# A Fourier-and-MLP layer on one core: block 8, the first transform and all product units in a new hand-written order

## The chip, the core and the metric

The kernel runs on one NeuronCore of a Trainium2 chip. The core has five engines that run side by side and meet only at semaphores: TensorE (PE in the profile, with its weight loads as PEld), VectorE (DVE), ScalarE (ACT), GpSimd (POOL) and SyncE (SP). Each engine takes its instructions strictly in the order in which they were written for it. DMAs are started by an instruction on SP, ACT or POOL and then run by themselves. The metric is device time in microseconds: 1245.67 us is the median of three runs of the kernel before (1245.28 to 1251.84).

## The reference

```python
def _A_ref(x, dft_seq_re, dft_seq_im, dft_hid_re, dft_hid_im):
    a = jnp.einsum("bsd,ed->bse", x, dft_hid_re)
    b = jnp.einsum("bsd,ed->bse", x, dft_hid_im)
    y = jnp.einsum("ts,bse->bte", dft_seq_re, a) - jnp.einsum("ts,bse->bte", dft_seq_im, b)
    return y

def _B_ref(x, w1, w2):
    h = jnp.einsum("bsd,df->bsf", x, w1)
    zero = jnp.zeros_like(h)
    h = jnp.maximum(h, zero)
    return jnp.einsum("bsf,fd->bsd", h, w2)

x = A_x
xn = _layernorm(x, axis=-1)
return x + _A_ref(xn, A_dft_seq_re, A_dft_seq_im, A_dft_hid_re, A_dft_hid_im) + _B_ref(xn, B_w1, B_w2)
```

x is 2048 x 576 in float32, the hidden size of the MLP is 4608, the Fourier matrices are 2048 x 2048 and 576 x 576 (real and imaginary part of each). A layer norm, a two-dimensional Fourier transform written as matrix products, and an MLP with relu are added to x.

## The kernel before

**Numbers.** Every float32 operand is split in a high and a low float16 part, and a product is three float16 products (high x high, high x low, low x high). Before it is split it is scaled by a power of two that is found from its largest magnitude. The large products use a seven-product scheme (Strassen-Winograd) on 2 x 2 blocks, so there are sums of operand blocks to make before the products and sums of product blocks after them.

**Stages.** (1) The start (BLOCK0): x is loaded tile by tile, normalised, split and transposed, and MLP block 0 is computed. (2) MLP blocks 1 to 8 of 512 hidden columns (BLOCK1, BLOCK, BLOCK8), each in four steps of 512 tokens: step t = 4b+g is block b, token group g, so steps 32 to 35 are block 8. Partial outputs are added to a spill area in device memory by DMAs from POOL. (3) The hidden transform: the normalised x times the 576 x 576 Fourier matrix gives the right-hand operands R (16 row blocks, first 0 to 7, later 8 to 15). (4) Sixteen units multiply blocks of the 2048 x 2048 matrices with R: units 0 to 7 with rows 0 to 7, units 8 to 15 with rows 8 to 15. Between units 7 and 8 stands the second half of the hidden transform (TURN).

**What sets the order.** BLOCK0, BLOCK1, BLOCK, BLOCK8 and TURN are strings of words; run and run_block take them one by one, each calling a function that emits a few instructions, and in a hand-written stretch every engine has its instructions in the order of the words. Units 1 to 6 and 9 to 15 are not in the strings: the function unit emits them in a loop, outside the hand-written stretch, and the framework's planner orders them for each engine. Unit 0 is in BLOCK8; units 7 and 8 are in TURN.

**The words.** In an MLP block: `p:t:i:k` is product k of step t, pair i (7 matmuls, L663); `f` copies a product's bank out (ACT L653 or DVE L655, by the tag :A or :V, L685 to L689 where it adds); `h`, `l`, `r`, `x`, `y`, `H`, `L` make relu, sums and the high and low parts of the hidden values (L672 to L710); `m:t:q` is product q of the second weights (12 matmuls, L760); `e` evicts it (L774 on ACT, L776 on DVE, or L778 where it adds); `a` is the DMA that adds it to the spill area (POOL, L785). `F` loads a block of the large Fourier matrix for its scale (SP, L1164, one buffer for all) and `S` has ACT sum its magnitudes (L1171), so an F waits for the S before it.

For the 576 x 576 matrix: `dl` and `dx` load its four quarters and find their maxima, `dR` and `dp` make the scale, and `dL:z:k` loads part k of its real (z=0) or imaginary (z=1) half again (L1105 to L1123). k is 0 or 1 for the main rows and 2 for the last 64 rows; a last part is eight small DMAs on SP (L336, L337), the others are four (L1121). Parts go to two buffers in turn, except dL:1:2, which goes to free columns of dbuf and accs. `dh` (ACT, L1135) and `dw` (DVE, L1141) make high and low parts, `ds` (DVE, L878 to L881) sums.

In the transform: `q:t:z:n` is product n (7 matmuls, L1321), `c` collects it (L1334, L1336, L1338), `rs` makes the sums (L1300 to L1303), `sh` and `sl` the high and low parts of R (ACT L1290, DVE L1294).

In unit n: `u:n:i:0` and `u:n:i:1` are the halves of product i (12 matmuls each, L1414), `cl:n:q` loads block q of its left operand (SP, L1354), `os` sums blocks (DVE, L1376), `oh:m` and `ol:m` split operand m = 7n+i (ACT L951, DVE L955), `ue` evicts (ACT L1428, DVE L1426 or L1430), `ua` sends a result off: in units 0 to 7 by a POOL DMA that adds to the spill area (L1438), in units 8 to 15 by a store from SP (L1442). `lo` reloads the partial outputs (SP, L1402). The left operand has two sets of buffers, by n odd or even; so have the outputs, by the unit's row p.

**The start.** The first weights' half i=0 is loaded in two halves of three DMAs each, all from SP, between the first and the second tile of x (L973, L974 call load_w1_main and load_w1_rest).

Of the kernel before, what the change touches and what calls it, by code (L numbers as in the profile page):

```python
# [146 lines left out]
f:32:1:5:V h:32:0:12 H:32:0 l:32:0:12 a:31:1 dx:2:0 f:32:1:7 L:32:0 m:31:3 p:33:0:1 p:32:1:3
p:32:1:4 p:33:0:2 e:31:3:A h:32:1:11 h:32:1:22 f:32:1:3 f:33:0:1:V m:31:5 r:32:1 e:31:2:A
h:32:1:12 x:32:1 m:31:4 p:33:0:5 p:33:0:6 e:31:5 dx:2:1 e:31:4 y:32:1 l:32:1:22 S:33:0
f:33:0:5:V m:31:6 f:33:0:6:V l:32:1:12 l:32:1:11 p:33:0:3 p:33:0:7 dl:3 F:33:1 f:33:0:2 e:31:6:A  # L150
f:33:0:7 dx:3:1 f:33:0:3 p:33:1:1 p:33:0:4 p:33:1:2 m:32:0 dx:3:0 h:33:0:11 h:33:0:22 H:32:1
h:33:0:12 dR:0 a:31:4 a:31:5 a:31:6 S:33:1 dL:0:0 f:33:1:1:V e:32:0:A r:33:0 dL:0:1 m:32:1
# [12 lines left out]
p:35:0:6 r:34:1 e:33:4 f:35:0:2 dw:0:2:2 x:34:1 f:35:0:6:A dh:0:2:3 p:35:0:5 f:35:0:5:V S:35:0
m:33:5 m:33:6 p:35:0:7 p:35:1:2 dw:0:2:3 e:33:6:A y:34:1 e:33:5 l:34:1:11 l:34:1:12 dL:1:0
F:35:1 dL:1:1 f:35:0:7 a:33:4 p:35:0:3 p:35:1:1 p:35:0:4 m:34:1 f:35:0:3 f:35:1:1:V p:35:1:6
m:34:0 H:34:1 h:35:0:11 h:35:0:22 r:35:0 p:35:1:5 x:35:0 f:35:1:2 y:35:0 L:34:1 f:35:1:6:V
l:35:0:22 p:35:1:7 H:35:0 h:35:0:12 h:35:1:11 e:34:0:A L:35:0 f:35:1:5:V l:35:0:11 p:35:1:3
f:35:1:7 f:35:1:3 e:34:1 p:35:1:4 m:34:2 a:33:5 a:33:6 m:34:3 r:35:1 dh:1:0:0 dh:1:1:0 e:34:2:A  # L170
l:35:0:12 x:35:1 h:35:1:12 dh:1:0:1 dh:1:1:1 e:34:3:A dh:1:2:1 dh:1:2:0 S:35:1 m:34:4 y:35:1
a:34:1 dw:1:0:0 dw:1:1:0 l:35:1:11 e:34:4 dw:1:2:1 m:34:5 dw:1:0:1 e:34:5 l:35:1:12 m:34:6
dw:1:1:1 m:35:0 ds:1:0 ds:1:1 h:35:1:22 e:34:6:A a:34:4 a:34:5 a:34:6 H:35:1 e:35:0:A dh:1:0:2
dh:1:1:3 m:35:1 L:35:1 q:0:0:1 q:0:0:5 e:35:1 l:35:1:22 m:35:2 m:35:3 dh:1:1:2 pm:0 dw:1:2:0
e:35:2:V e:35:3:A a:35:1 m:35:4 ds:1:2 e:35:4 dw:1:1:2 m:35:5 e:35:5 m:35:6 dh:1:2:2 dh:1:0:3
e:35:6:A dh:1:2:3 fs:0 a:35:5 a:35:6 a:35:4 dw:1:2:2 dw:1:0:3 dw:1:1:3 dw:1:0:2 q:0:0:2 q:0:1:1
q:1:0:1 fm:0 cl:0:0 c:0:1:1:V c:0:0:5:A c:0:0:1:A c:0:0:2 dw:1:2:3 q:0:1:2 q:0:1:6 q:0:0:6 pa:0
pb:0 c:0:1:6:A sh:0:11 sl:0:11 c:0:1:2 q:0:1:5 q:0:1:7 c:0:1:5:A c:0:0:6:V q:0:0:3 pc:0 c:0:1:7
c:0:0:3 pd:0 q:0:1:3 q:0:0:7 q:0:1:4 q:1:1:1 c:0:1:3 sh:0:21 sh:2:11 c:1:0:1:A sl:0:21 c:0:0:7
q:0:0:4 sh:2:22 sh:2:21 c:0:1:4:A sl:2:11 q:1:1:5 sl:2:21 sh:0:22 sl:2:22 q:1:0:2 q:1:0:6  # L180
sl:0:22 q:1:1:2 rs:2 c:1:1:1:A c:0:0:4:A c:1:1:5:A rs:0 q:1:1:3 q:1:1:6 sh:2:0 sh:0:0 c:1:1:6:A
c:1:0:6:A sl:2:0 q:1:0:5 q:1:1:7 c:1:0:5:A c:1:1:2 sl:0:0 c:1:1:7 q:1:0:3 q:1:0:7 sh:3:22
# [1381 lines left out]
```

## Time and profile before

| | us |
|---|---|
| median of three runs (lowest, highest) | 1245.67 (1245.28, 1251.84) |
| the profiled execution | 1249.48 |
| its span, first to last instruction | 1247.6 |
| PE busy | 1215.2 |
| DVE busy | 1050.8 |
| ACT busy | 726.4 |
| POOL busy | 214.7 |

The profile is of one execution; its times are microseconds from the first instruction. Block 8 runs from about 700 to 810 us, the first transform to about 866, units 0 to 7 to about 1022, the second transform to about 1074, and the last units to the end. "idle before, releaser" names what ended an engine's wait. The granted clock is the share of TensorE's full clock that the chip allowed; below 1.00 a matmul takes longer, and PE counts as busy all the same.

### The profile page before, as it was taken

The numbers are of one execution on the slowest core, as the hardware profiler recorded it, in microseconds if no ns is written. First come the engines' busy times: TensorE is split into PE (matmuls) and PEld (weight loads), VectorE is DVE, ScalarE is ACT, GpSimd is POOL, SyncE is SP. The second block draws the span as 40 slices with busy tenths as digits, with TensorE's granted clock in tenths as the row PEclk, the third lists the DMA queues.
The fourth block names the chain that finished last, engine by engine and source line by source line (L and its number), as shares of the span: only waits on it lengthen the run. The fifth ranks groups of instructions, "written<-read, shape, count | busy, mean of one in ns | idle before, by whom it ended". The sixth has DMA issues, their size and how long they took to land.

```text
span 1247.6 us, 26034 instructions
## 1 busy us (share of the span) xinstructions
PE 1215.2 (97%) x10394; PEld 995.8 (80%) x10394; DVE 1050.8 (84%) x2029; ACT 726.4 (58%) x1273; POOL 214.7 (17%) x279
## 2 busy tenths in 40 slices
PE   6999999999999999999999998999999999999998
PEld 6856778888888888888888886876777777777777
DVE  7977999988898889888998787989787669887775
ACT  6765776766756667657666565655444445534332
POOL 2651112222122122212111111200111110000000
PEclk9999999999999999999999998999999999999999
DMA  7997568688878777777676776642555631345431
GB/s 224 202 184 169 166 137 162 158 152 158 164 143 166 152 144 163 137 142 162 135 128 136 168 171 137 107 97 72 160 130 132 137 80 42 118 136 180 137 120 34
DMA packets 127051, 175.96 MB, mean 141 GB/s; under 512 B 48337, under 2 KB 88785, under 8 KB 126929
## 3 DMA queue, kind: packets, MB, share of 16 engines
q1 hardware_dynamic: 98256, 122.38, 34.1%
q0 software_dynamic: 28672, 51.92, 28.9%
q8 instruction: 81, 1.33, 0.4%
q14 instruction: 42, 0.34, 0.1%
HBM read 112.53 MB, written 56.62 MB: 136 GB/s over the span
## 4 chain that ended last, share of the span: by engine, by line
PE 75%; DVE 9%; DMA 7%; issue 4%; ACT 2%; POOL 1%; SPq 1%; ACTq 0%; DVEq 0%; POOLq 0%
PE bank L663 25%; PE p L760 24%; PE p L1414 18%; PE pd L1321 7%; DMA out_dram<-accs 2%; DVE cs L955 2%; DMA accs<-in_x_dram 1%; DMA tb<-in_cim_dram 1%; PE p L539 1%; PE p L800 1%; DVE R L1294 1%; DVE accs L1426 1%; DMA f<-in_cim_dram 1%; DMA x<-in_x_dram 0%; DMA f<-in_cre_dram 0%
## 5 line engine op out<-in xcount | busy, mean ns | idle before, releaser
L760 PE MATMUL p<-w2s,h 128*128 128x288 f16 x2688 | 358.2, 286 | 0.8 <-ACT dbuf L774 0.6
L1414 PE MATMUL p<-R,cs 128*128 128x288 f16 x2688 | 332.9, 287 | 7.1 <-DVE accs L1426 3.9
L1414 PEld LDWEIGHTS <-cs 128*128 128x128 f16 x2688 | 263.7, 98 | 75.6 <-issue 8.5
L760 PEld LDWEIGHTS <-h 128*128 128x128 f16 x2688 | 263.3, 98 | 63.6 <-issue 1.1
L663 PEld LDWEIGHTS <-wbuf 128*128 128x128 f16 x1568 | 154.4, 98 | 25.6 <-issue 4.5
L663 PEld LDWEIGHTS <-dbuf 128*128 128x128 f16 x1568 | 153.2, 98 | 24.8 <-issue 4.7
L663 PE MATMUL bank<-xT,wbuf 128*128 128x256 f16 x896 | 112.1, 276 | 4.3 <-ACT s L653 4.3
L951 ACT ACTIVATE cs<-tb,sc_c 128x1024 f16<-128x1024 f32 x56 | 63.4, 1146 | 89.9 <-PE p L1414 57.0
L663 PE MATMUL bank<-xT,dbuf 128*128 128x256 f16 x896 | 109.9, 273 | 1.2 <-ACT accs L653 1.0
L785 POOL DMA_DIRECT2D spill<-dbuf x70 | 61.5, 928 | 165.6 <-DVE dbuf L778 123.2
L663 PE MATMUL bank<-accs,dbuf 128*128 128x256 f16 x672 | 85.9, 273 | 2.4 <-DVE accs L687 1.7
L955 DVE SCALAR_TENSOR_TENSOR cs<-tb,sc_c,cs 128x1024 f16<-128x1024 f32 x56 | 71.1, 1280 | 20.1 <-ACT cs L951 19.7
L663 PE MATMUL bank<-accs,wbuf 128*128 128x256 f16 x672 | 85.8, 273 | 0.0
L710 DVE TENSOR_TENSOR h<-s,h 128x1024 f16<-128x1024 f32 x64 | 77.3, 1216 | 1.8 <-ACT h L704 1.8
L951 ACT ACTIVATE cs<-accs,sc_c 128x1024 f16<-128x1024 f32 x40 | 45.1, 1144 | 54.3 <-PE p L1414 28.7
L704 ACT ACTIVATE h<-s 128x1024 f16<-128x1024 f32 x64 | 66.5, 1049 | 11.3 <-DVE s L701 11.3
L1171 ACT ACTIVATE f<-f 128x1024 f32<-128x1024 f32 x64 | 67.2, 1049 | 4.1 <-DMA f<-in_cre_dram 3.5
L774 ACT ACTIVATE dbuf<-p,c_ub 128x576 f32<-128x576 f32 x63 | 46.4, 737 | 35.1 <-PE p L760 35.1
L672 ACT ACTIVATE h<-accs 128x256 f16<-128x256 f32 x128 | 51.0, 409 | 25.2 <-DVE accs L687 22.8
L785 POOL DMA_DIRECT2D spill<-wbuf x42 | 39.8, 947 | 147.1 <-DVE wbuf L778 119.0
L653 ACT ACTIVATE accs<-bank 128x256 f32<-128x256 f32 x101 | 38.3, 379 | 46.0 <-PE bank L663 19.6
L955 DVE SCALAR_TENSOR_TENSOR cs<-accs,sc_c,cs 128x1024 f16<-128x1024 f32 x40 | 51.0, 1280 | 12.1 <-ACT cs L951 11.8
(224 smaller groups left out, 1886.8 us busy)
## 6 DMA issues: line engine op xcount, KB each, us to landing
spill<-dbuf POOLq DMA_DIRECT2D x80, 288.0 KB, 4.6
f<-in_cre_dram SPq DMA_DIRECT2D x32, 512.0 KB, 4.5
f<-in_cim_dram SPq DMA_DIRECT2D x32, 512.0 KB, 5.2
spill<-wbuf POOLq DMA_DIRECT2D x48, 288.0 KB, 5.5
raw_w<-in_w_dram SPq DMA_DIRECT2D x18, 576.0 KB, 4.7
raw_w<-in_w_dram SPq DMA_DIRECT2D x17, 512.0 KB, 4.6
accs<-in_cim_dram SPq DMA_DIRECT2D x16, 512.0 KB, 5.1
tb<-in_cre_dram SPq DMA_DIRECT2D x16, 512.0 KB, 4.6
```

Of the source, the lines that this page charges most:

```text
L663: nc.tensor.matmul(ps, l, r, start=first and m == 0, stop=m == len(todo) - 1, skip_group_check=not first,)
L672: nc.scalar.activation(next(high_low(q)), SOURCE[q], AF.Relu)
L704: order["s"] = nc.scalar.activation(next(high_low(SUMS)), stage_of(slice(1, 5)), AF.Copy).ins
L710: order["lo"] = nc.vector.tensor_tensor(lo, stage_of(slice(1, 5)), hi, ALU.subtract).ins
L760: nc.tensor.matmul(ps[:, c], h[:, x, qa, c * P : (c + 1) * P], w[:, y, qb], start=first and i == 0 and j == 0, stop=i == NQ - 1 and j == 2 ...
L774: freed(nc.scalar.activation(o, ps, AF.Copy, scale=us[b]))
L785: nc.gpsimd.dma_start(spill[g, row, col], sums[g, row, col], accum_op=ALU.add)
L951: nc.scalar.activation(hi, src, AF.Copy, scale=s)
L955: nc.vector.scalar_tensor_tensor(lo, src, s, hi, ALU.mult, ALU.subtract)
L1171: nc.scalar.activation(f, f, AF.Abs, scale=2.0**-10, accum_out=sums_c[:, n, q : q + 1])
L1321: nc.tensor.matmul(ps, x[:, k, c * P : (c + 1) * P], dsp[z][:, a, y], start=first and m == 0, stop=m == len(PASSES) - 1, skip_group_check= ...
L1414: nc.tensor.matmul(ps, w[:, a, RANK[k]], r[:, c, RIGHT[rq]], start=first and k == 0 and j == 0, stop=k == HK - 1 and j == 2, skip_group_ch ...
```

## The change

The words of BLOCK8 and TURN are put in another order. No product, sum, split or DMA of them is added or taken away, but some copies and evictions change engine between ACT and DVE. The words for units 1 to 6 are added to BLOCK8, and those for units 9 to 15 to TURN, in place of the loops over unit, which goes away with the function operand. dL:1:2 stood ahead of F:34:0 and is now behind F:34:1. One half of the first weights is loaded from ACT's queue. Two functions, total_w1 and cast_w1, and three names for words (ms, mc, rm) are added; no word of this kernel uses them, nor the prefix 0 that the second run function now takes.

```diff
-L:32:1 p:33:1:6 dL:1:2 l:33:0:22 l:33:0:12 dp:0 x:33:0 f:33:1:2 F:34:0 e:32:1 p:33:1:5
...
-h:34:0:11 ds:0:1 h:34:0:22 e:33:0:A l:34:0:22 l:34:0:11 e:32:6:A r:34:0 h:34:0:12 x:34:0 F:34:1
-dL:0:2 p:34:1:5 p:34:1:6 dh:0:2:1 dh:0:2:0 f:34:1:6:A f:34:1:5:A dh:0:1:3 a:32:5 a:32:6 m:33:1
...
-c:5:0:7 rs:4 q:5:0:3 sh:6:0 c:5:1:7 c:5:0:2 sh:5:21 c:5:1:3 q:5:0:4 q:5:1:4 sh:7:22 sh:4:0
-sh:7:21 fx:1 c:5:0:3 c:5:1:4:A sh:5:11 c:5:0:4:A sl:6:0 sl:4:0 sl:5:11 sl:7:22 sh:7:11 sh:5:22
-sl:5:22 sl:5:21 sl:7:21 sl:7:11 rs:5 oh:2 sh:5:0 oh:3 u:0:0:0 u:0:0:1 u:0:1:0 rs:7 ol:2 sl:5:0
-u:0:1:1 sh:7:0 ue:0:0:A sl:7:0 ol:3 os:0:3 u:0:2:0 u:0:2:1 ue:0:2:A oh:4 u:0:3:0 os:0:2 ol:4
...
+dh:0:0:3 f:34:0:5:V a:32:6 dw:0:0:2 m:33:1 dw:0:0:3 S:34:0 f:34:0:2 dL:0:2 p:34:0:3 f:34:0:6:V
+dw:0:1:0 e:33:0:A p:34:0:7 y:33:1 h:34:0:11 e:33:1 H:33:1 p:34:1:2 f:34:0:7 a:33:1 p:34:1:1
+l:34:0:11 h:34:0:22 L:33:1 p:34:0:4 F:34:1 f:34:1:1:A p:34:1:6 f:34:1:2 h:34:0:12 f:34:0:3
+h:34:1:11 ds:0:1 m:33:2 r:34:0 m:33:3 e:33:2:A f:34:1:6:V dL:1:2 x:34:0 dh:0:1:3 m:33:4 dh:0:2:1
+l:34:0:12 e:33:3:A y:34:0 dw:0:1:3 dh:0:1:2 m:33:5 e:33:4 H:34:0 l:34:0:22 a:33:4 dh:0:2:0
...
+c:5:1:3 rs:6 sh:7:21 u:0:0:0 sh:5:21 q:5:0:5 sl:5:21 sh:6:0 c:5:1:7 sl:4:0 q:5:1:4 sh:7:22
+c:5:0:5:A c:5:1:4:A q:5:0:3 sl:6:0 sh:5:22 c:5:0:7 c:5:0:3 q:5:0:4 sl:5:22 sh:7:11 sl:7:22
+sl:7:11 c:5:0:4:A fx:1 sl:7:21 oh:2 u:0:0:1 rs:5 oh:3 u:0:1:0 ue:0:0:A rs:7 sh:5:0 u:0:1:1 ol:2
+sh:7:0 sl:5:0 u:0:2:0 sl:7:0 ol:3 u:0:2:1 cl:1:3 cl:1:1 cl:1:0 os:0:3 cl:1:2 u:0:3:0 oh:6
...
+u:8:2:1 cl:9:0 cl:9:1 cl:9:3 ol:60 cl:9:2 u:8:3:0 cl:10:2 oh:62 ue:8:1 ue:8:2 u:8:3:1 ol:62
...
+u:9:0:1 ol:66 u:9:1:0 ue:9:0 os:9:3 cl:10:3 u:9:1:1 oh:67 cl:11:0 lo:2 u:9:2:0 ue:9:1 oh:68
+ol:67 u:9:2:1 ol:68 u:9:3:0 ue:9:2 oh:69 os:10:0 ua:9:2 u:9:3:1 ol:69 cl:11:2 u:9:4:0 ue:9:3
+oh:70 ol:70 u:9:4:1 os:10:1 u:9:5:0 oh:71 ue:9:4 cl:11:1 ol:71 ua:9:4 u:9:5:1 os:10:2 u:9:6:0
+oh:72 ue:9:5 ol:72 ua:9:5 u:9:6:1 u:10:0:0 ue:9:6 oh:73 cl:11:3 ua:9:6 ol:73 u:10:0:1 os:10:3
+u:10:1:0 ue:10:0 oh:74 cl:12:0 u:10:1:1 ol:74 u:10:2:0 lo:3 oh:75 os:11:0 u:10:2:1 ol:75 ue:10:1
...
-    def load_w1_rest(b, i, r):
+    def load_w1_rest(b, i, r, eng=nc.sync):
...
-        nc.sync.dma_start(dst[:size], bass.AP(src.tensor, src.offset, both))
-        nc.sync.dma_start(dst[size:], src[: 2 * RH].rearrange("(h p) f -> p h f", h=2))
+        eng.dma_start(dst[:size], bass.AP(src.tensor, src.offset, both))
+        eng.dma_start(dst[size:], src[: 2 * RH].rearrange("(h p) f -> p h f", h=2))
...
     for half in range(2):
-        load_w1_main(0, 0, slice(half, half + 1))
-        load_w1_rest(0, 0, half)
+        eng = (nc.sync, nc.scalar)[half]
+        load_w1_main(0, 0, slice(half, half + 1), eng)
+        load_w1_rest(0, 0, half, eng)
...
-    def unit(n):
-        p, kh = units[n]
-        if kh and p + 1 < NP:
-            load_out(p + 1)
-        for i in range(7):
-            m = n * 7 + i
-            block_product(n, i, slice(0, HK))
-            block_evict(n, i)
-            if i == 0 and n + 1 < nu:
-                for q in (0, 2, 1, 3):
-                    load_c(n + 1, q)
-            if m + AHEAD < 7 * nu:
-                operand(m + AHEAD)
-            block_out(n, i)
...
     run(BLOCK8, turn)
-    end_hand()
-    for n in range(1, HK - 1):
-        unit(n)
-    begin()
     run(TURN, turn)
     end_hand()
-    for n in range(HK + 1, 2 * HK):
-        unit(n)
```

More of the change, by code (lines that the diff above doesn't have):

```diff
@@ L147 @@
[L147 to L152, printed above, removed]
@@ L165 @@
[L165 to L170, printed above, removed]
@@ L171 @@
[L171 to L182, printed above, removed]
@@ new lines @@
+h:35:0:22 f:35:0:3 L:34:1 r:35:0 p:35:0:4 p:35:1:5 e:34:1 h:35:0:12 S:35:1 m:34:2 x:35:0 a:34:1
+y:35:0 dL:1:1 m:34:3 l:35:0:22 e:34:2:A f:35:1:1:V f:35:1:2 H:35:0 l:35:0:12 pm:0 m:34:4
+e:34:3:A L:35:0 h:35:1:11 f:35:1:5:A p:35:1:6 e:34:4 p:35:1:3 l:35:1:11 f:35:1:6:A a:34:4
+p:35:1:7 f:35:1:3 r:35:1 m:34:5 f:35:1:7 x:35:1 h:35:1:22 p:35:1:4 e:34:5 m:34:6 l:35:1:22
+dh:1:2:0 a:34:5 y:35:1 h:35:1:12 dw:1:2:0 dh:1:1:1 m:35:0 dh:1:0:1 e:34:6:V dh:1:1:0 l:35:1:12
+a:34:6 dh:1:0:0 m:35:1 dh:1:2:1 dw:1:1:1 dw:1:1:0 H:35:1 dw:1:2:1 dw:1:0:1 q:0:0:1 e:35:0:A
@@ new lines @@
+oh:11 u:1:1:1 cl:3:0 ol:11 u:1:2:0 oh:12 ue:1:1 ua:1:1 ol:12 u:1:2:1 cl:2:3 u:1:3:0 ue:1:2:V
+oh:13 ol:13 cl:3:2 u:1:3:1 u:1:4:0 ue:1:3:V oh:14 ol:14 u:1:4:1 os:2:0 u:1:5:0 oh:15 cl:3:1
+ue:1:4 os:2:1 ua:1:4 u:1:5:1 ol:15 u:1:6:0 oh:16 ue:1:5 os:2:2 ua:1:5 u:1:6:1 ol:16 cl:3:3
+u:2:0:0 oh:17 ue:1:6:V ua:1:6 ol:17 u:2:0:1 os:2:3 u:2:1:0 ue:2:0:A oh:18 cl:4:0 u:2:1:1 os:3:0
+u:2:2:0 ol:18 oh:19 ue:2:1 u:2:2:1 ol:19 ua:2:1 u:2:3:0 oh:20 cl:4:2 ue:2:2:A ol:20 u:2:3:1
+u:2:4:0 oh:21 ue:2:3:A ol:21 u:2:4:1 cl:4:1 os:3:1 u:2:5:0 oh:22 ue:2:4 ol:22 ua:2:4 u:2:5:1
@@ L198 @@
+ue:6:0:V oh:46 u:6:1:1 os:7:0 ol:46 u:6:2:0 oh:47 ue:6:1 u:6:2:1 ol:47 ua:6:1 u:6:3:0 ue:6:2:V
+oh:48 ol:48 u:6:3:1 u:6:4:0 ue:6:3:A oh:49 u:6:4:1 ol:49 u:6:5:0 ue:6:4 oh:50 os:7:1 ua:6:4
+u:6:5:1 ol:50 u:6:6:0 ue:6:5 oh:51 ua:6:5 ol:51 u:6:6:1 ue:6:6:A ua:6:6
 """
@@ new lines @@
+q:12:1:6 c:9:1:4:A sh:9:22 q:12:1:5 c:12:1:6:A sl:9:22 sh:11:0 rs:9 q:12:1:2 c:12:1:5:A q:12:0:5
+q:13:0:1 c:12:1:2 sh:9:0 sl:11:0 q:13:0:2 c:12:0:5:A sh:12:21 q:12:0:2 sl:9:0 q:12:0:6 sl:12:21
+c:13:0:1:A c:12:0:2 q:12:1:7 c:12:0:6:A c:13:0:2 sh:12:11 q:12:0:3 sh:13:11 c:12:1:7 sl:12:11
+sh:14:22 q:12:1:3 c:12:0:3 sl:14:22 sh:14:11 q:13:1:1 c:12:1:3 sl:13:11 sh:14:21 q:13:1:2
+sl:14:11 c:13:1:1:A sl:14:21 q:12:0:7 c:13:1:2 sh:13:21 q:12:1:4 c:12:0:7 rs:14 q:12:0:4
+c:12:1:4:A sh:12:22 q:13:1:5 c:12:0:4:A q:13:0:5 sl:12:22 c:13:1:5:A sl:13:21 sh:14:0 rs:12
@@ new lines @@
+u:10:3:0 oh:76 cl:12:2 ue:10:2 ua:10:2 ol:76 u:10:3:1 u:10:4:0 ue:10:3 oh:77 ol:77 u:10:4:1
+cl:12:1 os:11:1 u:10:5:0 oh:78 ue:10:4 ol:78 ua:10:4 u:10:5:1 os:11:2 u:10:6:0 oh:79 ue:10:5
+ol:79 u:10:6:1 cl:12:3 ua:10:5 u:11:0:0 ue:10:6 oh:80 ua:10:6 ol:80 u:11:0:1 os:11:3 u:11:1:0
+ue:11:0 oh:81 cl:13:0 os:12:0 u:11:1:1 lo:4 ol:81 u:11:2:0 oh:82 ue:11:1 ol:82 u:11:2:1 u:11:3:0
+ue:11:2 oh:83 cl:13:2 ua:11:2 ol:83 u:11:3:1 u:11:4:0 ue:11:3 oh:84 ol:84 u:11:4:1 cl:13:1
+os:12:1 u:11:5:0 oh:85 ue:11:4 ol:85 ua:11:4 u:11:5:1 os:12:2 u:11:6:0 oh:86 ue:11:5 ol:86
@@ L846, in max_w1, with total_w1, cast_w1 @@
             nc.vector.tensor_reduce(m, mx["f", b, i], AX.X, ALU.max)
+    def total_w1(i):
+        if ("w1", 0) not in mx:
+            mx["w1", 0], sc["w1", 0], pw["w1", 0] = cell("mw1"), cell("sw1"), cell("pw1")
+        mx["f", 0, i] = cell("mf", 1)
+        junk = w1bufs[i].bitcast(F16)[:, : 4 * 3 * P].rearrange("p (q k f) -> p q k f", q=4, k=3)
+        nc.scalar.activation(
+            junk, raws["w1", 0, i], AF.Abs, scale=2.0**-10, accum_out=mx["f", 0, i]
+        )
+    def cast_w1(i):
+        m = mx["b", i] = small.tile([P, 1], BF16, tag=f"mb{i}", name=f"mb0_{i}")
+        nc.vector.tensor_copy(m, mx["f", 0, i])
     def power_w1(b, i):
@@ L1065 @@
         "rw": lambda i: sum_w2(1, i),
+        "rm": lambda _: next(steps1.setdefault(3, power_w2(1)), None),
         "f": fill,
@@ L1224, in run_block @@
             name, at, *args = word.split(":")
+            if name[0] == "0":
+                run(word[1:], act)
+                continue
             at = int(at) + (b if name in by_block else b * NG)
@@ L1385, in operand_of @@
         return w[:, 0], w[:, 1], src, sc["c"][:, n : n + 1]
-    def operand(m):
-        n, i = divmod(m, 7)
-        for k in {S2: (0, 1), S3: (3,), S4: (2,)}.get(PRODUCTS[i][0], ()):
-            sums_of(n, k)
-        split(*operand_of(m))
     def place(p, h):
```

140 lines of the change are left out of this document (88 added, 52 removed).

## The prediction

> **What bounds the kernel now.** I read the page first, then busy time in stretches of 25 us, then the chain of waits and the timelines around each stretch in which TensorE is not full. The page:
>
> ```profile
> span 1247.6 us, 26034 instructions
> PE 1215.2 (97%) x10394; PEld 995.8 (80%) x10394; DVE 1050.8 (84%) x2029; ACT 726.4 (58%) x1273; POOL 214.7 (17%) x279
> ```
>
> TensorE (PE) is busy 97% and sets the time; 32.4 us of the span is not PE work, and a new order of the same work can only win there (or where PE runs at a lower clock). The stretches with such time that the change touches (columns: us, PE, PE weight load, DVE, ACT, POOL busy, granted clock, DMA share, GB/s):
>
> ```profile
> 0.00:25.00 25.00, 14.46 (x194) 13.54 (x195) 18.73 (x71) 14.86 (x23) 5.27 (x19) 1.00 0.81 216
> 750.00:775.00 25.00, 20.68 (x156) 16.31 (x154) 16.21 (x33) 12.01 (x25) 2.56 (x3) 0.86 0.60 131
> 825.00:850.00 25.00, 25.00 (x206) 19.97 (x205) 23.53 (x44) 15.75 (x34) 0.00 (x0) 1.00 0.19 65
> 850.00:875.00 25.00, 21.94 (x165) 16.65 (x164) 23.61 (x40) 14.45 (x22) 0.00 (x0) 0.93 0.35 106
> 1100.00:1125.00 25.00, 23.56 (x193) 18.56 (x191) 19.52 (x22) 9.81 (x9) 0.00 (x0) 1.00 0.52 150
> 1125.00:1150.00 25.00, 24.67 (x203) 19.58 (x201) 20.43 (x23) 9.29 (x9) 0.00 (x0) 1.00 0.56 169
> 1150.00:1175.00 25.00, 24.89 (x204) 19.74 (x203) 19.61 (x22) 9.88 (x9) 0.00 (x0) 1.00 0.52 159
> 1175.00:1200.00 25.00, 24.15 (x199) 19.15 (x196) 17.07 (x20) 9.44 (x9) 0.00 (x0) 1.00 0.52 164
> 1200.00:1225.00 25.00, 23.73 (x195) 18.83 (x193) 21.36 (x24) 9.08 (x8) 0.00 (x0) 1.00 0.16 49
> ```
>
> So four places: the start (10.5 us idle), block 8 at 750 (4.3 us, clock 0.86), the end of the first transform at 850 (3.1 us, clock 0.93), and units 9 to 15 (1.44+0.33+0.11+0.85+1.27 = 4.0 us).
>
> **Part A: block 8, the Fourier matrix's last part.** SP's timeline, the wait behind its first row, PE's wake-up, and the chain of waits:
>
> ```profile
> 744.64 0.34 SPq L336 DMA_DIRECT2D dbuf<-in_dft_dram  x1
> 747.82 0.42 SPq L337 DMA_DIRECT2D accs<-in_dft_dram  x1
> SPq L336 <- DMA spill<-dbuf: 8.3, 1, 8.3
> 765.60 4.64 PE L663 MATMUL bank<-xT,wbuf 128*128 128x256 f16 x21 [4.32 <-ACT s L653]
> 748.35 5.29 DMA f<-in_cre_dram
> 754.83 6.40 DMA f<-in_cim_dram
> 761.25 2.75 DMA raw_dk<-in_dft_dram
> 770.24 2.08 PE p L760 x12
> 772.31 0.77 PE bank L663 x7
> 773.08 1.47 PE p L760 x12
> 774.55 2.29 PE bank L663 x21
> ```
>
> The step dL:1:2 (eight DMAs, 744.64 to 748.24, into dbuf and accs) waits 8.3 us for block 7's spill out of dbuf. On SP, which issues in order, F:34:0, F:34:1 and dL:0:2 queue behind it; ACT waits for each F, and at last for dL:0:2 at 764.0; behind that ACT wait stand the bank copies (L653) that PE needs. PE loses 4.32 us, then runs slowly: 21 matmuls take 4.64 instead of 2.29, and 12 take 2.08 instead of 1.47. Together 4.32+2.35+0.61 = **7.3 us**.
>
> After, dL:1:2 is moved behind F:34:0, dL:0:2 and F:34:1, when the spill is long over, so its eight issues (3.6 us of SP) delay only F:35:0; its first reader dh:1:2:0 comes after all remaining products of step 34 and most of 35, over 20 us later. What is late next is dL:0:2: it now goes right after dw:0:0:3 frees its buffer, and ACT first reads it (dh:0:2:1) behind e:33:2. PE has six products (0.77) and one m (1.47) before that eviction, 6.1 us, and ACT's two steps ahead (the eviction and a part of the same 576 columns, by DVE's 0.81 for the same eviction, quoted below) add 1.6: 7.7 us of lead, against 3.6 of issuing plus 2.75 of landing = 6.4. It fits by 1.3 us; each us over this is a us of ACT, with the evictions e:33:3 and the copies of step 35 behind it.
>
> DVE pays for the new order. It takes three copies and four first evictions from ACT (the tags :V rise from 12 to 15 on f and from 2 to 6 on e):
>
> ```profile
> L655 DVE COPY accs<-bank 128x256 f32<-128x256 f32 x27 | 11.2, 417 | 0.8 <-PE bank L663 0.6
> L776 DVE TENSOR_SCALAR dbuf<-p,c_ub 128x576 f32<-128x576 f32 x7 | 5.7, 810 | 0.0
> 764.65 0.51 DVE L1141 SCALAR_TENSOR_TENSOR dbuf<-raw_dk,c_sd,dbuf 32x288 f16<-32x288 f32 x1 [5.12 <-ACT dbuf L1135]
> 700.00:810.10 110.10, 105.55 (x881) 87.24 (x880) 91.10 (x188) 60.84 (x115) 17.61 (x22) 0.97 0.68 143
> ```
>
> 3 x 0.417 + 4 x 0.810 = 4.5 us more on DVE: 91.1+4.5 = 95.6 us in a stage that is to shrink from 110.1 to 102.8. DVE must then be 93% busy. It does run at 23.53 of 25 (94%) from 825 to 850, at which 95.6 us take 101.7. Here, A's own 5.12 us of DVE wait left out, it was busy 91.1 of 105.0 (87%), at which they take 110.2 and the gain is gone. I take 1.0 us off, near the good end, because the same engine packs its work so in the next stage. Part A: **6.3**, ends -0.1 and 7.3.
>
> **Part B: the transform's tail.**
>
> ```profile
> 860.63 3.35 PE L1414 MATMUL p<-R,cs 128*128 128x288 f16 x26 [0.88 <-DVE R L1294]
> 866.15 14.08 PE L1414 MATMUL p<-R,cs 128*128 128x288 f16 x100 [2.18 <-ACT accs L1428]
> 855.75 4.83 DVE L1294 TENSOR_TENSOR R<-tb,R 128x1152 f16<-128x1152 f32 x8
> 865.38 2.62 DVE L1294 TENSOR_TENSOR R<-tb,R 128x1152 f16<-128x1152 f32 x2
> 866.00:868.00 2.00, 1.85 (x11) 1.29 (x11) 2.00 (x3) 0.10 (x1) 0.00 (x0) 0.73 0.18 23
> 868.00:870.00 2.00, 2.00 (x11) 1.25 (x9) 1.97 (x3) 0.00 (x0) 0.00 (x0) 0.50 0.85 250
> ```
>
> PE idles 0.88+2.18 = 3.06 us and then loses 2 x (0.27+0.50) = 1.5 at the low clock: 4.6 us at stake. Last in line is DVE: after its last collect (855.75) it still does eight low parts (4.83, waits in it), two sets of sums, a low operand and two wide low parts, to 868.0. The new order leaves four low parts instead of eight behind that collect (about 1.5 us), then the same (868.00-860.58 = 7.4 us, of which ACT's interludes are few): 8.9 us. PE has q:5:0:4 (7 matmuls of 0.1225 us, 1.47 over 12) and four half products of unit 0 (1.47 each) to cover it: 6.7. About 2.2 us stay uncovered, where 3.06 were; ue:0:0 is no longer behind sh:7:0 on ACT, but DVE ends last, not ACT. Gain 0.9 if the clock still drops, 2.4 if it doesn't; a DVE that arrives later than before costs up to 1. I take **1.5**, between the two, ends -1 and 4.6.
>
> [...]
>
> **Part C: the units.** The chain of waits, SP's waits, and a load's landing:
>
> ```profile
> 1102.77 5.23 DMA out_dram<-accs
> 1108.86 5.84 DMA tb<-in_cim_dram
> 1123.38 20.63 PE p L1414 x167
> SPq L1402 <- DMA out_dram<-accs: 32.5, 13, 4.5
> tb<-in_cim_dram SPq DMA_DIRECT2D x16, 512.0 KB, 5.3
> ```
>
> In units 9 to 15 SP holds, in order, the reload of partial outputs (L1402), which waits up to 4.5 us for the store of the same buffer, and behind it the next unit's Fourier blocks (L1354). They land late, DVE's sums of them wait, and behind these on DVE stand the evictions (L1426) for which PE waits: the 4.0 us above. By hand, the blocks of unit n+2 are issued within unit n and ahead of the reload: cl:10 stands in unit 8, cl:11:0 before lo:2. The latest, cl:11:3, is behind the store that needs ue:9:5, so it goes some 1.3 us into u:9:6; its reader os:11:0 is on DVE in u:10:2: six half products of 1.47 less 1.3 = 7.5 us, against 5.3 of landing. The waits on stores stay on SP but nothing needed soon is behind them. Units 1 to 7 have no idle PE to win. Gain **4.0**, ends -1 (a stall by hand where the planner had none) and 4.0.
>
> **Part D: the start.** Three of the six DMAs of the first weights go from SP to ACT, so x's next tile is issued earlier:
>
> ```profile
> 4.13 1.38 SPq L297 DMA_DIRECT2D accs<-in_x_dram  x3
> 4.76 0.29 ACT L433 ACTIVATE u<-mv,eps 128x1 f32<-128x1 f32 x1 [2.54 <-DVE mv L428]
> 2.00:4.00 2.00, 0.00 (x0) 0.00 (x0) 1.45 (x7) 0.21 (x2) 0.00 (x0) 1.00 0.90 297
> ```
>
> Three issues of about 0.46 (1.38 for three) are 1.4 us; on ACT they lie in its 2.54 us wait (without it they would delay the first root by 1.4). But the DMA engines are 90% busy from 2 us on, and the first x tile now shares them with the second half of the weights. Gain 1.4 if issuing was the limit, a loss of 0.5 if x comes later; I take **0.3**, as 90% busy is nearly full. [...]
>
> New functions for the maximum of the first weights are called by no word: 0. The end (last eviction and store after the last matmul) stays.
>
> **Sum:** 6.3+1.5+4.0+0.3 = 12.1. The profiled execution took 1249.48 (its span and 1.9 around it): 1237.4. It is 3.8 above the median of the runs shown, so on that scale 1245.67-12.1 = **1233.6**.
>
> **Rivals.**
> 1. Everything goes: 7.3+4.6+4.0+1.4 = 17.3, **1228.4**. For: each wait has a named cause that the order removes. Against: B is DVE's own load.
> 2. DVE becomes the bound of block 8: it packs at its 87%, so A is worth 0, and it comes late to the transform, B -1; C 4.0 and D 0.3 are left: 3.3, **1242.4**. For: 4.5 us more work on it. Against: the 94% seen at 825.
> 3. It doesn't do what it says: a part of the Fourier matrix still lands late, for want of the 1.3 us in A, and ACT stalls there as before; only C's 4.0 and D's 0.3 are won: **1241.4**.
> 4. Slower: hand-written units stall. One mechanism: DVE's sums of unit n+1 stand ahead of evictions of unit n; if a block lands later than its 7.5 us of lead, every one of 14 units loses what the worst did before, 1.44: 20.2 us, 1245.67-12.1+20.2 = **1253.8**. It decides once landing takes 2.2 us more than the 5.3 seen. Against: two units' loads are spread over more time than before.
>
> **Numbers.** Forecast 0.55, rivals 0.15, 0.14, 0.08, 0.08. About 0.5% (6.2 us, below 1239.4) is what can be told from no change. Faster: the forecast (all but 0.03 of it) and rival 1, with 0.05 of rivals 2 and 3 that may come out better, 0.72; slower: rival 4, 0.08; same the rest, 0.20. The range 1227.5 to 1241.5 holds the forecast (1229 to 1239 by itself), most of rival 1 and half of rivals 2 and 3, and leaves out rival 4.
>
> **What would show it.** A: no PE idle over 1 us between 740 and 800, clock 1.00 there, and dL:1:2 issued without the spill wait. B: PE idle of some 2 us before the second half of product 2 of unit 0, released by DVE R. C: PE full from unit 8 to the last product; SP's waits on stores still there. D: the first product with the first weights within 0.5 us of where it was. Wrong would be: PE waits released by DVE evictions in step 33 to 35, or any in units 1 to 7.

## The result and the profile after

| | before | after |
|---|---|---|
| median (lowest to highest) of 8 executions each, us | 1245.62 (1242.78 to 1251.84) | 1238.11 (1236.09 to 1239.47) |
| the profiled execution, its span | 1249.48, 1247.6 | 1237.58, 1235.8 |
| PE busy; the rest of the span | 1215.2; 32.4 | 1211.6; 24.2 |
| DVE busy | 1050.8 | 1061.7 |

The ratio is 0.9931, with a 95% interval of 0.991 to 0.9952: 8.6 us less (6.0 to 11.2); the medians differ by 7.5. In the experiments below two executions, one of before at 1276.44 us and one of the second edit of experiment 5 at 2589.24, ran far slower than all others and are left out of ratios and means. The forecast was 12.1 less, 1233.6; it came out 1238.1. Between the two *profiled* executions, though, the gain is 11.9. Why the same change is worth 11.9 in one comparison and 7.5 in the other is the main question below.

The page of the kernel after, its span and first row of busy times:

```profile
span 1235.8 us, 26013 instructions
PE 1211.6 (98%) x10394; PEld 993.7 (80%) x10394; DVE 1061.7 (86%) x2046; ACT 722.7 (58%) x1256; POOL 213.6 (17%) x279
```

The rest of the span fell by 8.2 us, and PE's busy time by 3.6 with the same 10394 matmuls: that part is the clock, whose mean over the span was 0.996 before and 0.999 after. Busy time by stretches of 25 us in the kernel after (columns as in the prediction):

```profile
750.00:775.00 25.00, 25.00 (x219) 21.19 (x217) 24.08 (x54) 16.62 (x30) 5.12 (x6) 1.00 0.81 161
775.00:800.00 25.00, 25.00 (x212) 20.59 (x211) 24.12 (x48) 15.79 (x29) 4.27 (x5) 1.00 0.68 132
825.00:850.00 25.00, 24.99 (x205) 19.82 (x203) 24.28 (x47) 16.66 (x33) 0.00 (x0) 1.00 0.19 65
850.00:875.00 25.00, 21.63 (x172) 16.29 (x170) 24.72 (x33) 13.48 (x18) 1.71 (x2) 1.00 0.49 155
1100.00:1125.00 25.00, 25.00 (x206) 19.96 (x204) 20.49 (x24) 10.34 (x9) 0.00 (x0) 1.00 0.49 162
1200.00:1225.00 25.00, 25.00 (x207) 19.97 (x205) 18.16 (x20) 9.19 (x8) 0.00 (x0) 1.00 0.07 25
```

A's stretch (750) is full at clock 1.00, where PE had 20.68 us at 0.86. C's stretches (1100 to 1225) are full. B's stretch (850) has no less idle than before, 3.37 us against 3.06, but its clock no longer drops. DVE is busy 96% from 750 to 800 and 99% at 850. The waits in B, PE's timeline of the kernel after (bracket: idle before, and what released it):

```profile
852.54 1.02 PE L1389 MATMUL pd<-dbuf,accs 128*128 128x288 f16 x7 [0.79 <-DVE tb L1402]
859.27 3.18 PE L1475 MATMUL p<-R,cs 128*128 128x288 f16 x24 [1.05 <-DVE cs L1017]
863.00 3.11 PE L1475 MATMUL p<-R,cs 128*128 128x288 f16 x24 [0.55 <-DVE cs L1017]
867.01 9.24 PE L1475 MATMUL p<-R,cs 128*128 128x288 f16 x74 [0.90 <-DVE cs L1017]
```

Four short waits took the place of two longer ones. L1017 is the low part of a left operand (ol), L1402 a collect; none is released by R, which the forecast had named. And SP's timeline after, around dL:1:2 (L383 and L384 are L336 and L337 of before, L1229 is L1164):

```profile
745.80 0.33 SPq L1229 DMA_DIRECT2D f<-in_cre_dram  x1
755.56 0.34 SPq L383 DMA_DIRECT2D raw_dk<-in_dft_dram  x1
...
759.34 0.37 SPq L1229 DMA_DIRECT2D f<-in_cim_dram  x1
759.82 0.42 SPq L383 DMA_DIRECT2D dbuf<-in_dft_dram  x1
...
764.78 0.31 SPq L384 DMA_DIRECT2D accs<-in_dft_dram  x1
```

The order is as planned: F:34:0, dL:0:2, F:34:1, then dL:1:2.

### The profile page after: what moved, and what is told of

It reads as the page before. It is cut to its first block, busy times and chain, and to the rows that moved or that the text cites. A ratio compares the mean times of both kernels' runs of the same rounds, so it can differ in the third digit from the quotient of the medians.

```text
span 1235.8 us, 26013 instructions
## 1 busy us (share of the span) xinstructions
PE 1211.6 (98%) x10394; PEld 993.7 (80%) x10394; DVE 1061.7 (86%) x2046; ACT 722.7 (58%) x1256; POOL 213.6 (17%) x279
## 4 chain that ended last, share of the span: by engine, by line
PE 87%; DVE 6%; DMA 2%; issue 2%; ACT 1%; POOL 1%; SPq 1%; POOLq 0%; DVEq 0%; ACTq 0%
PE bank L710 26%; PE p L807 26%; PE p L1475 26%; PE pd L1389 7%; PE p L847 1%; PE p L586 1%; DMA raw_w<-in_w_dram 1%; DVE R L1362 1%; DMA accs<-in_x_dram 1%; DMA x<-in_x_dram 0%; DMA xT<-wbuf 0%; DVE st L471 0%; DVE wbuf L923 0%; ACT dbuf L511 0%; DVE cs L1017 0%
## 5 line engine op out<-in xcount | busy, mean ns | idle before, releaser
L1017 DVE SCALAR_TENSOR_TENSOR cs<-tb,sc_c,cs 128x1024 f16<-128x1024 f32 x56 | 71.7, 1283 | 22.2 <-ACT cs L1013 21.4
L1017 DVE SCALAR_TENSOR_TENSOR cs<-accs,sc_c,cs 128x1024 f16<-128x1024 f32 x40 | 51.2, 1281 | 13.7 <-ACT cs L1013 13.3
```

Of the source, the lines that this page charges most:

```text
L1017: nc.vector.scalar_tensor_tensor(lo, src, s, hi, ALU.mult, ALU.subtract)
```

## The experiments

Times of a kernel are compared with those of the kernel before on the same chip; "us" behind a ratio is that ratio of some 1245.5. For each execution its mean granted clock is known to 0.001; (1 - clock) x span is taken as what it lost at low clock, an estimate from rows like the prediction's, in which 21 matmuls took 4.64 us at clock 0.50 and 2.29 at full clock. One such value is coarse (steps of 1.2 us), a mean over many is not.

**1. The kernel before once more.**

> The kernel before, unchanged, profiled a second time. Theory 1 (the idle is fixed, the clock is not): PE idle near 4.3 us at 750-775, 3.1 at 850-875 and 4.0 in units 9 to 15 as in the first profile, but the clock that is granted after the first two differs, so that the 3.0 us (2.35+0.61) and 1.5 us that PE lost at a low clock there come out elsewhere between 0 and these; the execution lies between 1243 and 1250 with them. Theory 2 (the profiled execution is typical): the same losses again within 0.5 us each, and then the profile's gain of 11.9 should also be that of the medians, which it is not (7.5).

It took 1243.06. Busy time by stretches:

```profile
750.00:775.00 25.00, 21.57 (x174) 17.55 (x173) 18.32 (x37) 13.97 (x29) 3.36 (x4) 0.93 0.67 156
850.00:875.00 25.00, 21.94 (x165) 16.65 (x164) 22.77 (x36) 13.77 (x20) 0.00 (x0) 0.93 0.41 132
1100.00:1125.00 25.00, 24.08 (x198) 19.11 (x196) 19.92 (x22) 10.79 (x10) 0.00 (x0) 1.00 0.54 168
```

A's idle is 3.43 where it was 4.32, B's 3.06 as before, and units 9 to 15 idle 0.92 us, all in the stretch shown, where they idled 4.0. Theory 2 falls. Of theory 1 the half on the clock holds: the stretch at 750 loses 1.75 us to it (0.07 of 25) where it lost 3.5. The half on the idle doesn't: idle that ends on a DMA differs between executions of one program too. The 4.0 us that the forecast took for C were one execution's. The five profiles here with the old units 9 to 15 give 4.00, 0.92, 1.55, 1.28 and 2.12 us, mean 2.0.

**2. A alone.**

```diff
-L:32:1 p:33:1:6 dL:1:2 l:33:0:22
+L:32:1 p:33:1:6 l:33:0:22
-dL:0:2 p:34:1:5 p:34:1:6 dh:0:2:1
+dL:0:2 dL:1:2 p:34:1:5 p:34:1:6 dh:0:2:1
```

> The kernel before with the one step dL:1:2 moved behind F:34:1 and dL:0:2 (no work changes engine, all else as before). Theory 1 (what counts is the idle): about 4.3 us less, 1241, with no idle over 1 us of PE at 750-775. Theory on record (idle and clock loss): 7.3 less, 1238, since the 4.5 us of extra DVE work is not in it. Rival (the wait goes to dL:0:2, which stays right ahead of its reader in the old order): under 2 us less, and ACT idle of some 3 us behind the DMA of dL:0:2.

Ratio 0.996 (0.9946 to 0.9975): 5.0 us less (3.1 to 6.7), which leaves out the 7.3 on record. The timeline of ACT, then that of PE:

```profile
760.83 1.20 ACT L1135 ACTIVATE dbuf<-raw_dk,c_sd 128x288 f16<-128x288 f32 x2 [4.83 <-DMA raw_dk<-in_dft_dram]
```

```profile
762.35 2.45 PE L663 MATMUL bank<-xT,wbuf 128*128 128x256 f16 x21 [2.34 <-ACT s L653]
```

The spill wait is gone from SP, but ACT still waits 4.83 us for dL:0:2, whose reader stands right behind it in the old order, and PE still idles 2.34 us. The rival's mechanism is there; its price was wrong, since no low clock follows the shorter idle here (21 matmuls take 2.45, not 4.64).

**3. A undone in the kernel after.**

```diff
-m:32:5 l:33:1:12 dh:0:0:0 f:33:1:3 F:34:0
+m:32:5 l:33:1:12 dh:0:0:0 f:33:1:3 dL:1:2 F:34:0
-e:33:2:A f:34:1:6:V dL:1:2 x:34:0
+e:33:2:A f:34:1:6:V x:34:0
```

> The changed kernel with dL:1:2 put back right ahead of F:34:0. Theory 1 (A is its idle of 3.4 to 4.3 us and, in most executions, 1 to 3 us at a low clock): 4 to 7 us slower than the changed kernel, 1242 to 1245, with a PE idle of over 3 us at 750-775 behind an ACT wait. Rival (the new order of the other words has more lead and hides it): under 2 us slower, 1240 at most.

Median 1237.65, ratio 0.9937 (0.9921 to 0.9953): as fast as the kernel after. The rival holds, against theory 1 and against the prediction. SP's timeline, and ACT's:

```profile
744.40 0.36 SPq L383 DMA_DIRECT2D dbuf<-in_dft_dram  x1
...
748.13 0.38 SPq L1229 DMA_DIRECT2D f<-in_cre_dram  x1
755.20 0.31 SPq L383 DMA_DIRECT2D raw_dk<-in_dft_dram  x1
...
758.43 0.42 SPq L384 DMA_DIRECT2D raw_dk<-in_dft_dram  x1
```

```profile
754.42 1.06 ACT L1236 ACTIVATE f<-f 128x1024 f32<-128x1024 f32 x1 [0.56 <-DMA f<-in_cre_dram]
...
762.02 1.19 ACT L1200 ACTIVATE dbuf<-raw_dk,c_sd 128x576 f16<-128x576 f32 x2
```

The same two places of ACT's timeline in the kernel before, then the last of dL:0:2's eight DMAs there on SP:

```profile
753.66 1.06 ACT L1171 ACTIVATE f<-f 128x1024 f32<-128x1024 f32 x1 [3.49 <-DMA f<-in_cre_dram]
...
764.08 1.20 ACT L1135 ACTIVATE dbuf<-raw_dk,c_sd 128x288 f16<-128x288 f32 x2 [6.55 <-DMA raw_dk<-in_dft_dram]
```

```profile
761.25 0.31 SPq L337 DMA_DIRECT2D raw_dk<-in_dft_dram  x1
```

SP issues dL:1:2 and F:34:0 no later and no earlier than in the kernel before, within 0.3 us (744.64 and 748.35 there), but ACT asks for the data with more work ahead of it: it waits 0.56 us for F:34:0 instead of 3.49, and none for dL:0:2 instead of 6.55. So in the new order the place of dL:1:2 makes no difference. Three of the order's other changes bear on this wait. ACT's readers of dL:0:2 come later: ACT gets to them at 762.02, in the kernel before at 757.53 (764.08 less its wait of 6.55). dL:0:2 stands ahead of F:34:1 and no longer behind it, and the last of its eight DMAs goes out at 758.43 instead of 761.25. And the two copies f:34:1:5 and f:34:1:6, which stood behind these readers on ACT, are on DVE. No run takes the three apart.

**4. The readers on ACT later, alone and with dL:1:2 moved.**

```diff
-dL:0:2 p:34:1:5 p:34:1:6 dh:0:2:1 dh:0:2:0 f:34:1:6:A
+dL:0:2 p:34:1:5 p:34:1:6 f:34:1:6:A
-m:33:2 S:34:1 dh:0:1:2 y:34:0
+m:33:2 S:34:1 dh:0:1:2 dh:0:2:1 dh:0:2:0 y:34:0
```

> The kernel before with dL:1:2 where it was; only ACT's two steps that read dL:0:2 (dh:0:2:1 and dh:0:2:0) moved five words of ACT later, behind dh:0:1:2, so that two copies (f:34:1:6, f:34:1:5), one part and one sum of magnitudes come first. Theory (what cost PE the idle at 765 is that this reader stands ahead of PE's copies, whatever makes the load late): PE's idle there falls from 3.4 to 4.3 us to under 1.5, and 3 to 5 us are won, 1241. Rival (the spill wait ahead of F:34:0 is the cause, as the forecast had it): the idle only moves, at most 1 us is won.

> The kernel before with both: dL:1:2 behind dL:0:2, and the two readers of dL:0:2 behind dh:0:1:2. Theory: no PE idle over 0.5 us at 750-800, against 2.3 us with dL:1:2 moved alone, and 5 to 7 us less than before, 1239. Rival (the two do the same thing): as with either alone, 5.0 less.

Alone: 0.999 (0.9978 to 1.0002), nothing won; with dL:1:2 moved: 0.9964 (0.9948 to 0.9979), 4.5 us less, no more than A alone. Both theories failed, and both rivals had the outcome right. The timeline of DVE, then of PE, with the readers alone:

```profile
766.81 0.51 DVE L1141 SCALAR_TENSOR_TENSOR dbuf<-raw_dk,c_sd,dbuf 32x288 f16<-32x288 f32 x1 [4.77 <-ACT dbuf L1135]
```

```profile
767.70 2.51 PE L663 MATMUL bank<-xT,wbuf 128*128 128x256 f16 x14 [3.64 <-DVE accs L685]
```

The wait went to the next engine: dw:0:2:1, DVE's half of the same step, had stayed where it was, and PE's accumulations (L685) are queued behind it. With both edits PE idles 1.03 us, released by DVE's L685 again (2.33 in the profile of experiment 8, which has both too). The new order has dh and dw later; no run has that pair in the old order.

**5. Units 9 to 15: by hand, and SP's order alone.** The first is the kernel before with the new TURN and without the last loop over unit. The second:

```diff
         p, kh = units[n]
-        if kh and p + 1 < NP:
-            load_out(p + 1)
...
                     load_c(n + 1, q)
+            if i == 0 and kh and p + 1 < NP:
+                load_out(p + 1)
```

> The kernel before with the new TURN alone, units 9 to 15 by hand. The forecast's part C: 4.0 us less, 1241.6, PE full from unit 8 to the last product. Rival 4 (hand-written units stall): slower by 1 us or more.

> The kernel before with one order changed in the function unit: the reload of the partial outputs is issued behind the next unit's four Fourier blocks instead of ahead of them; the planner still orders the rest. If SP's order is the cause of the idle in units 9 to 15, this alone wins 3 to 4 us, 1242, as much as the hand order. If the hand order of DVE and ACT is what matters, under 1 us.

By hand: 0.9982 (0.997 to 0.9994), 2.2 us less (0.7 to 3.7). SP's order alone: 0.9993 (0.9979 to 1.0008), 0.9 less, not told from nothing. In both profiles PE is full over these units, and in all others with the hand order too; a stretch of the one by hand:

```profile
1100.00:1125.00 25.00, 25.00 (x206) 19.97 (x205) 21.35 (x24) 10.56 (x10) 0.00 (x0) 1.00 0.60 182
```

C's cause was right, its size half of what was forecast: 2.2, in line with the mean idle of 2.0. SP's order alone takes all of PE's idle in its profile and, by its time, anything from 2.6 us to nothing; whether the hand order adds to it, these intervals don't tell.

**6. D undone** (`eng = nc.sync` for both halves in the kernel after).

> The changed kernel with all of the first weights on SP again. First weight products so far at 17.69, 15.86, 16.84, 16.46 and 16.97 us in five executions with the start of before (mean 16.8), at 16.31 in the one of after. Theory (D is worth 0.3, lost in the start's own spread): within 1 us of the changed kernel's 1238, the first weight product at 16 to 18 us. Rival (D saves the issue time): 1.4 us slower, the first product 1.4 later than 16.3.

Median 1237.26, ratio 0.9936 (0.9919 to 0.9953): no difference in time. PE's row of the first products with the first weights, after and undone:

```profile
16.31 0.94 PE L586 MATMUL p<-xT,wbuf 128*128 128x128 f16 x14
```

```profile
16.59 0.94 PE L586 MATMUL p<-xT,wbuf 128*128 128x128 f16 x14
```

Over all profiles of this study it comes at 16.24 on average with half the weights on ACT's queue (five, 16.06 to 16.39) and at 16.65 without (nine, 15.79 to 17.69): 0.4 us, where 0.3 was forecast, but the nine alone spread over 1.9 us.

**7. What sets the tail of the transform.** Three edits to the kernel after: six DVE instructions of step 34, 35 and the transform on ACT (tags :V to :A); two early sums of unit 0 on GpSimd; and the order in the tail itself:

```diff
-        tt(o, a, b, op)
+        (nc.gpsimd.tensor_tensor if (n, k) in ((0, 0), (0, 1)) else tt)(o, a, b, op)
```

```diff
-c:5:0:5:A c:5:1:4:A q:5:0:3 sl:6:0 sh:5:22 c:5:0:7 c:5:0:3
+c:5:0:5:A c:5:1:4:A q:5:0:3 sh:5:22 c:5:0:7 sl:6:0 c:5:0:3
-ue:0:2:V
+ue:0:2:A
-ue:0:3:V
+ue:0:3:A
+        terms = [(k, a, c) for k in range(HK)[ks] for a, c in ((0, 0), (0, 1), (1, 0))]
+        if n == 0:
+            late = (lambda t: t[2]) if ks.start else (lambda t: t[1])
+            terms.sort(key=late)
```

> The changed kernel with two first evictions (e:34:0, e:34:6), two copies (f:35:0:6, f:35:1:1) and two collects (c:0:0:1, c:0:1:5) moved from DVE to ACT: 2 x 0.81 + 2 x 0.417 + 2 x 0.452 = 3.4 us less of DVE between 765 and 825. Theory 1 (the transform's tail idles because DVE, full since 750, arrives late): nearly all of PE's 3.4 us of idle at 850-875 goes, 1235. Rival (ACT's sums in between or the order of the tail set it): the idle at 850-875 stays over 2.5 us and the time within 1 us of 1238.

> The changed kernel with the two sums os:0:0 and os:0:1 (1.22 us each on DVE at 838 and 840) on GpSimd, which is idle there. Theory 1 (DVE arrives late): 2.4 us less of idle in the tail, some 1 us left, 1236. Rival (these sums are late on GpSimd, 2.5 us each by its 1.27 for half the size, or slow DVE): the idle stays at 3 us or more, 1238 or slower.

> The changed kernel with, in unit 0 alone, the four matmuls of each half product that need DVE's last result (the low part of the left operand; in second halves that of R) put behind the other eight, c:5:0:7 ahead of the wide low part sl:6:0, and two evictions (ue:0:2, ue:0:3) on ACT. Theory (DVE alone, by its own work from 847 to 868, sets the tail; PE has 0.98 us more of each half product to run ahead on): idle at 850-875 falls from 3.37 to 1.5-2.5, 1 to 2 us won, 1237. Rival (PE only reaches the next wait sooner): idle moves to later halves, within 0.5 us of 1238.

Less work for DVE ahead of the tail: 1239.32, ratio 0.9952 (0.9933 to 0.9971), not faster. A stretch, and PE's timeline:

```profile
775.00:800.00 25.00, 24.91 (x209) 20.18 (x208) 21.29 (x42) 17.30 (x32) 4.26 (x5) 1.00 0.68 127
```

```profile
858.82 3.18 PE L1475 MATMUL p<-R,cs 128*128 128x288 f16 x24 [1.06 <-DVE cs L1017]
862.55 3.11 PE L1475 MATMUL p<-R,cs 128*128 128x288 f16 x24 [0.55 <-DVE cs L1017]
```

DVE did drop from 24.12 to 21.29 there, and the tail's waits stayed as they were to 0.01 us. So DVE doesn't carry a backlog into the tail. It still waits for PE's products later on (DVE's timeline after):

```profile
837.91 0.46 DVE L1402 SCALAR_TENSOR_TENSOR tb<-pd,tb 128x288 f32<-128x288 f32 x1 [0.26 <-PE pd L1389]
```

The run with less work has the same 0.26 us there, at 837.45, so in both DVE has caught up with PE by then. Most of the 2.8 us that it saved it had waited away before, 1.08 and 1.12 us at 782.79 and 792.52, for ACT, which now had the work. The sums on GpSimd: 1239.46, the same ratio, the tail's waits the same again, and one more ahead of them. PE's, GpSimd's, then DVE's timeline in that run:

```profile
839.39 1.02 PE L1389 MATMUL pd<-dbuf,accs 128*128 128x288 f16 x7 [1.22 <-ACT tb L1404]
```

```profile
835.12 2.50 POOL L1444 TENSOR_TENSOR accs<-accs 128x1024 f32<-128x1024 f32 x1 [29.16 <-DMA accs<-in_cim_dram]
837.69 3.35 POOL L1444 TENSOR_TENSOR c<-accs,c 128x1024 f32<-128x1024 f32 x1
```

```profile
835.74 3.09 DVE L1362 TENSOR_TENSOR R<-tb,R 128x1152 f16<-128x1152 f32 x1
...
839.71 1.65 DVE L1362 TENSOR_TENSOR R<-tb,R 128x288 f16<-128x288 f32 x1
...
847.37 0.46 DVE L1402 SCALAR_TENSOR_TENSOR tb<-pd,tb 128x288 f32<-128x288 f32 x1 [0.30 <-PE pd L1389]
```

The 2.4 us taken from DVE were lost at once, as its neighbours took 3.09 instead of 1.35 and 1.65 instead of 0.45, and PE waited 1.22 us more. Here DVE, though late, waits for PE as late as 847.37. From there to 868 it has no gap, so the tail is DVE's own work behind the last products. The third edit does move it; PE's timeline with the third edit:

```profile
861.08 2.01 PE L1478 MATMUL p<-R,cs 128*128 128x288 f16 x15 [1.06 <-DVE cs L1017]
863.61 3.33 PE L1478 MATMUL p<-R,cs 128*128 128x288 f16 x25 [0.52 <-DVE R L1362]
867.25 1.15 PE L1478 MATMUL p<-R,cs 128*128 128x288 f16 x8 [0.30 <-ACT cs L1013]
868.57 7.65 PE L1478 MATMUL p<-R,cs 128*128 128x288 f16 x61 [0.17 <-DVE cs L1017]
```

The idle is 2.05 instead of 3.3, as its theory had it. Which of the edit's three parts did it isn't told apart: besides the new orders, two evictions of 0.51 us have left DVE. In time that is 1237.74, ratio 0.9933 (0.9918 to 0.9947), too close to 1238.11 to call it faster than the kernel after.

**8. Three small edits to the kernel before:** A alone, the readers on ACT later, and the new TURN.

> The kernel before with three small edits: dL:1:2 behind dL:0:2, the readers of dL:0:2 later, and the new TURN with units 9 to 15 by hand; block 8's order, its division between DVE and ACT, units 1 to 6 and the start as before. Theory (A is worth 5 to 6, C 2.2, B and D nothing): 7 to 8 us less than before, as fast as the changed kernel. Rival (the rest of the new order matters): over 2 us slower than the changed kernel, 1240 or more.

Median 1238.62, ratio 0.9941 (0.9925 to 0.9958): 7.3 us less (5.2 to 9.3), not told apart from the kernel after. PE still idles 2.33 us at A in its profile. So most of what the change wins, at the least, needs neither the new order of block 8 nor the hand-written units 1 to 6.

## Why the prediction was right, and where it was wrong

**Direction and range** were right: 1238.1 lies in 1227.5 to 1241.5. The size was 4.5 us too large: 12.1 forecast, 7.5 measured.

**The step that failed is the size of the terms**, and with it the last step of the sum: 12.1, read from one execution, was taken off the median of 1245.67 instead of being left on the scale of that execution. On that scale the sum said 1237.4, and the kernel after took 1237.58 when profiled and 1238.1 in the median. The profiled execution of before stood 3.8 above its median, and the excess was not spread over all its work: it sat in the very terms that the change removes. A's idle was 0.4 above its mean (below), C's 2.0, and the clock cost 5.0 us (0.996 over the span) where the mean is 3.3; together that is 4.1. The executions, taken apart by their clocks:

| mean of | time | lost at low clock | the rest |
|---|---|---|---|
| 56 executions of before | 1245.7 | 3.3 | 1242.4 |
| 8 of after | 1238.1 | 0.8 | 1237.3 |
| 10 of A alone | 1240.2 | 0.7 | 1239.5 |
| 12 of the new TURN alone | 1243.5 | 3.3 | 1240.1 |

So the gain is 2.5 us of clock and 5.1 of the rest. The forecast counted 2.96 (A) and up to 1.5 (B) of clock, and 4.32 and 4.0 of idle in A and C, all read from the one profiled execution; in the mean it is 2.5 of clock in all, 3.9 for A's idle (4.32, 3.43, 3.57 and 4.22 in the four profiles with that code) and 2.0 for C's. Less the 0.3 by which B's idle grew, that makes 8.1, against 7.6 in the table.

That 1237.4 and 1237.58 lie so close is luck in part. Between the two profiled executions A gave 7.3 and not 6.3, B 1.2 (1.5 of clock less 0.3), C 4.0, and PE reached its matmuls at 90 us 0.8 earlier; but there the execution of after lost 1.7 to a low clock (last section), and that of before nothing. These make 11.6 of the 11.9.

**A, 6.3.** In the mean A is worth about this: 3.9 of idle, all of which went, and most of the 2.5 of clock. But two errors cancel in it: the profile's 7.3 was above the mean, and the 1.0 taken off for DVE was not paid. DVE ran at 96% in 750 to 800, above the 94% that the estimate used, and PE has no idle there. The cause was wrong, or rather half of one. The spill wait ahead of dL:1:2 was taken as the thing to remove; but moving dL:1:2 alone leaves 2.34 us of idle, and putting it back in the new order costs nothing. Moving ACT's readers of dL:0:2 alone leaves 3.64, both edits 1.03 and 2.33 in two profiles. The new order also has dL:0:2 ahead of F:34:1, DVE's readers later and two of the copies on DVE. Which of these is enough stays open.

**B, 1.5.** The idle was to fall from 3.06 to 2.2 and rose to 3.37. The step "DVE ends last, not ACT" was right on the engine, and the 8.9 us of DVE behind its last collect are there, from 852.85 to the end of the two wide low parts of R. But the forecast has one wait of PE, for these parts of R. PE waits for three low parts of left operands instead (L1017), which end at 859.21, 862.94 and 866.95; two of them stand behind that point, and the forecast left them out. DVE's timeline after:

```profile
859.13 2.62 DVE L1362 TENSOR_TENSOR R<-tb,R 128x1152 f16<-128x1152 f32 x2
861.66 1.28 DVE L1017 SCALAR_TENSOR_TENSOR cs<-accs,sc_c,cs 128x1024 f16<-128x1024 f32 x1
...
865.68 1.27 DVE L1017 SCALAR_TENSOR_TENSOR cs<-accs,sc_c,cs 128x1024 f16<-128x1024 f32 x1
```

DVE runs without a gap from 847 to 868, and each of its results that PE needs in that time is a little late. What B did win is clock: its waits are now 1.06 us at most and the clock stays at 1.00 in all six profiles with the new order; before, it fell in four of eight (last section).

**C, 4.0.** Right in cause, and full in effect (no PE idle left), but 2.2 in size: a wait that ends on a DMA was sized from one execution. One sign failed: SP's waits of the reload on the stores from accs, 32.5 us in the prediction's row, were to stay and are gone in the profile after. Rival 4 didn't come: no unit stalls.

**D, 0.3.** 0.4 at the first weight product in the mean, within the spread; 1.4 (17.69 to 16.31) between the two profiled executions, outside the 0.5 that the forecast allowed; in the time not seen. **The rivals.** Rival 1 would have needed B's idle to go. Rivals 2 and 3 fell: DVE is nearly full and still on time in block 8, and dL:0:2 is awaited by nobody.

## What to carry to other kernels

Size a wait that ends on a DMA, and any loss to a low clock, from several profiles of the unchanged kernel; where there is one profile only and it stands above the median, keep the sum on the profile's own scale. Before a load is moved, look at where its readers stand on *every* engine that takes part in the step: a reader that was moved on one engine alone handed the wait to the next. Work taken off a busy engine ahead of its last wait for the engine that is the bound won nothing here.
